# A second table of issue positions, and other engines for a dozen conversions and unit parts, in an mLSTM + MoE kernel

## The chip, the cores and the metric

The kernel runs on one core of one Trainium2 chip. The metric is device microseconds (us) of one execution, median over runs; the profile is one further execution taken by the hardware profiler, and every duration below is from it. Engines: PE (TensorE matmul; PEld its weight loads), DVE (VectorE), ACT (ScalarE), POOL (GpSimd), and SP (SyncE), which here issues DMAs only.

## The reference

Three stages follow one another on 1536 tokens (batch 2 x 768 positions) of width 320 (8 heads x 40).

```
# 1 attention, per batch and head, over t:
m_new = max(f[t] + m, i[t])
C = exp(f[t] + m - m_new) * C + exp(i[t] - m_new) * outer(v[t], k[t])
n = exp(f[t] + m - m_new) * n + exp(i[t] - m_new) * k[t]
y[t] = sigmoid(o[t]) * (C q[t]) / max(|n . q[t]|, 1)
# 2 one dense layer, w_in 320 x 2048, w_out 2048 x 320
h = x @ w_in
g = (a0 + a1 h + a2 h^2 + a3 h^3) / (1 + |b0| |h| + |b1| h^2 + 1e-6)
x = g @ w_out
# 3 four experts, w1 320 x 1024, w2 1024 x 320
out = sum over e of p[:, e] * (relu(x @ w1[e]) @ w2[e])
```

All is float32 outside; the weights of stage 2 arrive as 8-byte values.

## The kernel before, in words

**Attention** is done in 12 tiles (6 chunks of 128 positions x 2 batches). Each tile goes through steps that hang on one another: broadcast of the gates by a matmul (`bc`, `bf`, L415 and L470), a scan over them on DVE (`fb`, L536), the scores `sc` (PE, L566) times that decay (DVE, L571), the chunk's state `dl` (PE, L608 and L611) from `kend` and `v` (POOL and ACT, L554 to L582), the outputs `o` (PE, L590 and L596), a reciprocal of the denominator `den` (DVE, L598, L599 and L624), the output gate (POOL, L627; DVE, L631), and a transpose of the result (`tx`, PE, L651; its high and low halves by ACT L656 and DVE L657). The sigmoid of `o_gate` (tile `so`) is made on ACT from L480 on. All gates are first prepared by `gates1` (L383 to L421), whose scan at L400 needs `f_gate` and `i_gate`.

**The dense layer** is done in 48 units, 6 token groups x 8 pieces of the hidden width; a unit is 16 matmuls into `h` (128x256, L674), the rational function on 128x512 elements (`e_mono`), and 12 matmuls into `acc` (L703). The function takes two ACT operations at L721 and L722, `r = a3 h + a2` (ACT, L724, or DVE, L726), a sum on POOL or DVE (L727), DVE operations at L728, L729, L732, L733 and L734, ACT operations at L730 and L731, and a split of the result `s` into a high part `gh` (ACT, L258) and a low part `gl = s - gh` (L738, POOL or DVE). Every float32 operand of a matmul is split in two parts this way. Strings in the dictionary `KP` name the engine of each of these for each unit (`RI`, `SU`, `GLE`), and where two intermediate results lie (`UP`: P in PSUM, S in SBUF).

**The weights** of the dense layer come in 22 pieces of 512 KB, each a DMA into one of two staging buffers per matrix (`stg_a`, `stg_b`, issued at L315 to L329). A piece is converted from its 8-byte form by ACT (L286, L292), POOL (L298) and DVE (L300), and split into a high part (ACT, L258) and a low part (L267, on POOL or DVE by the string `LO`). The experts' weights are float32, staged as `stg_c` and `stg_d`, split likewise (L258, L262, L267). An expert's unit is 128x512 matmuls into `h`, a relu split on ACT (L743) and DVE (L744), and matmuls into `acc`; the first expert's units are partly laid between units of the dense layer.

**The order.** A step's instructions are traced in the order of emission times in `KP` (`T0`, `ST`, `MT`, `QT` and others). Behind the trace stands the table `ORDER`: for PE, DVE, ACT, POOL and SP a list of ranges of that engine's traced instructions. Each engine's listed instructions are chained in the list's order, so the table, not the trace, sets in what order they are issued; what is behind the table's end follows the scheduler of the framework:

```
for eng, text in ORDER.items():
    own = [i for i in traced if str(i.engine).split(".")[-1] == eng]
    ...
    for a, b in zip(seq, seq[1:]):
        tc.add_manual_dep(b, a.name, ...)
```

Each engine executes its list in order, so an instruction that waits holds up all behind it on that engine.

Of the kernel before, what the change touches and what calls it, by code (L numbers as in the profile page):

```python
# [27 lines left out]
278-293 344 338 345 339 346 340 347 341 348 342 349 343 267-268 306 269 307-309 367 310-325 356-357 350-351 358
352 359 353 360 354 361 355 368-372 389-412 362 413 382 387 421-438 414 383 439 415 388 363 440 384 441 364 442
373 365 416 366 374 443-444 463-478 375 445-446 501 447-448 502 534-539 378 417-418 479-481 419-420 454-458 379  # L30
459-461 380 506 482-497 510-513 449 540-541 498-500 507 542 450 508 543 451 544 452 518-528 509 529-530 453 531
545 532 462 551 533 552 503-505 585 591-592 586 514-517 553 561 554 569 593 570 594 562 555 571 565-568 595 572
563 556 573-574 564 557 575-576 596 558 577 587 578 559 546 579 560 580-582 588 583 589 584 590 630-633 648
547-548 608 634 549 609-610 550 611-612 624 613 625 614-616 597 626 617 635 649 627 618-619 628 600 620-621 601
622-623 602 629 603 598 636 599 637-642 650 643 651-653 604-607 654 662-663 655 684 664 656 665 685 666 657 686
667-668 687 669 688 670-673 689 674 644 675-676 678 677 679-682 645 647 646 683 727-730 696 731 697 732-734 755
698 735 699 736 658-661 700 737-739 718 756 740-741 719 701 742 690 714 691 715 692 716 693 760 694 717 720 761
721 762 695 722 763 723-726 764-766 772-773 767 774-776 708 777 831 709 778 710 779 711 780-781 712 782-785 713
786 832 787 702-707 749-750 743 751 744 833 752 745 834 746 757 768-771 800-802 808 803 809-812 804 813-814 805
815-816 806 817 747 835 807 818 758 748 819 836 820-823 759 753 788 754 794-795 789 837 796 838 797 790 798 839  # L40
791 799 827 792 840 793 828-830 860-861 824 862 825-826 863 892-894 841-856 895-899 857-859 880-891 919-920
864-872 900-901 873-874 902 875-879 925 921 926 922 927 923 928-929 903-916 924 917-918 930 947-948 953-954
949-950 955 951 956-957 952 931-932 958 933-937 959 938 960 939 961 940 962 941 963 942 964 943 965 944 966 945
967 946 968-976 981-982 977-978 983 979 984-985 980 1011-1013 986 1014-1026 987-988 993-994 989-990 995 991
# [12 lines left out]
1390 1318 1339 1391 1340 1392-1393 1341 1394 1324 1395 1342 1396 1343-1344 1347 1345 1348 1346 1369 1349 1370
1350-1351 1375-1376 1371-1373 1352 1374 1377-1380 1435-1436 1397 1419-1426 1400 1427 1401 1428 1398 1402 1429
1441 1403 1430 1399 1442 1431 1404 1437 1432 1405 1438 1433 1406 1434 1407 1439 1408-1412 1463 1443 1413 1464
1414 1465 1440 1415 1466 1469 1467 1470 1444 1471 1445 1472-1473 1468 1475-1477 1474 1478-1479 1446 1416 1480  # L60
1417 1481-1483 1418 1484-1490 1447-1462
    """,
    DVE="""
9-10 8 4 7 5 78 0-3 6 11-12 14 13 40 15 22 24 16 41 23 25 17 43 45 19 18 42 44 20 26-27 21 29 46 31 28 30 32
85-88 36-37 33 38 79 34 39 35 59 63 47 60 57 48 50 80 49 58 61 81 51 82 52 62 68 55 69 72 56 64 73 53-54 65-66
83 91-92 84 67 75 102 70 103 74 71 116 118 99 76-77 130 89 131 133 90 93 120 134 94 121 127 95 128 145 96 129 97
146 100 98 104 101 153 105-106 140-141 107 143 108-109 154 110 132 165 114 111 117 115 112 144 113 142 166 178
122-123 119 147 124 179 125 135 126 136 160 185 137 161 186 138 148 139 149 163 150-151 164 152 155 162 156-159
168 167 169-177 188-191 199 193 192 194 198 180-181 183 195 182 196 184 197 205 217 206 210 218 207 200 187 208
201 209 203 226 211 216 212 204 213 220 214 202 230 215 231 221 219 222 243 242 223-224 232 227 233 225 234 257  # L70
228 235 229 236-237 258 238-241 246 251 264 247 252 244-245 253 248 265 254 249-250 256 255 278 259-260 279
261-262 266 263 267 271 286 270 268 272 287 269 300 273 276 301 274 277 275 281-285 288-289 296 308 297 280 298
290 309 291 299 295 292-294 315-317 302 307 303 318 304-305 319 306 310-311 320 323 312 324 313-314 321 325-326
# [12 lines left out]
245-247 261-264 236 265-266 248 267-268 249 234 252-253 251 254-256 258 269-270 250 259 271 260 272-273 275-277
257 278-279 283-284 274 285 281 286-287 289 280 282 290-291 298 288 295 299 296 292 306 297 307 293 300-302 308
303 294 304 315-316 309-311 305 317 320 312 321-322 313 318 323 319 326 324 314 327-328 332-334 329 325 330
# [10 lines left out]
    """,  # L99
    SP="""  # L100
12 21 13 22 16 14-15 20 17-18 23 28-30 24-26 31 48 47 32-33 49 27 35 19 36-37 44-45 34 38-43 50-51 46 52 61-62
53 63 54 64-65 55-56 66 57-60 92 67-68 96 69 72 70-71 73-81 84 82-83 93-95 97-98
    """,
)


@with_exitstack
def kernel(
# [55 lines left out]
    YB, FB = KP["YB"], KP["FB"]  # L164
# [849 lines left out]
```

## Time and profile before

| | |
|---|---|
| median of 3 runs | 672.76 us (672.57 to 674.09) |
| the profiled execution | 671.89 us, its span 670.1 us |
| PE busy | 624.7 us (93%) |
| DVE busy | 379.1 us (57%) |
| ACT busy | 331.4 us (49%) |
| POOL busy | 233.8 us (35%) |

A row of engine windows gives a stretch, its length, and for each engine the busy time in it (with the count of instructions), then the granted PE clock (1.00 is full speed, 0.50 half), the mean busy share of the DMA engines, and GB/s. A row of a timeline gives start, duration, engine, line, operation, output and input, and in square brackets how long the engine had been idle and what released it. A busy PE need not be a PE at full speed: at half clock a matmul takes twice as long and counts as busy.

In this program the first 100 us hold the start, the conversion of the 22 pieces and the first tiles of attention; from 100 to about 251 us attention's later tiles and the dense layer's units run side by side; from there to about 405 us the dense layer and the first expert; the rest is the other three experts.

### The profile page before, as it was taken

The numbers are of one execution on the slowest core, as the hardware profiler recorded it, in microseconds if no ns is written. First come the engines' busy times: TensorE is split into PE (matmuls) and PEld (weight loads), VectorE is DVE, ScalarE is ACT, GpSimd is POOL, SyncE is SP. The second block draws the span as 40 slices with busy tenths as digits, with TensorE's granted clock in tenths as the row PEclk, the third lists the DMA queues.
The fourth block names the chain that finished last, engine by engine and source line by source line (L and its number), as shares of the span: only waits on it lengthen the run. The fifth ranks groups of instructions, "written<-read, shape, count | busy, mean of one in ns | idle before, by whom it ended". The sixth has DMA issues, their size and how long they took to land.

```text
span 670.1 us, 10411 instructions
## 1 busy us (share of the span) xinstructions
PE 624.7 (93%) x4120; PEld 590.5 (88%) x4120; DVE 379.1 (57%) x615; ACT 331.4 (49%) x618; POOL 233.8 (35%) x225
## 2 busy tenths in 40 slices
PE   2548789999999899999999999999999999999997
PEld 2447779999999899999999999999989999899997
DVE  6887898899988888767665522232222313313232
ACT  3987797876469976857867422111111111111111
POOL 4245677555447752223225994600000000000000
PEclk9568879999999999999999999999999999999999
DMA  8676651012105120000000542000000000001011
GB/s 217 194 196 193 191 161 41 1 53 67 41 1 132 37 87 1 1 1 1 1 1 1 156 143 61 20 1 1 0 1 1 1 0 1 1 1 39 1 40 39
DMA packets 15696, 35.65 MB, mean 53 GB/s; under 512 B 2048, under 2 KB 7424, under 8 KB 15648
## 3 DMA queue, kind: packets, MB, share of 16 engines
q1 hardware_dynamic: 15648, 35.00, 18.1%
q8 instruction: 32, 0.52, 0.3%
q14 instruction: 16, 0.13, 0.1%
HBM read 33.03 MB, written 1.97 MB: 52 GB/s over the span
## 4 chain that ended last, share of the span: by engine, by line
PE 81%; ACT 5%; POOL 4%; DVE 4%; issue 3%; DMA 3%; SPq 0%; DVEq 0%; ACTq 0%; POOLq 0%
PE h L674 38%; PE acc L703 35%; PE sc L566 2%; PE o L596 2%; DMA so<-in_o_gate_dram 2%; DMA stg_a<-in_moe_w_in_dram 1%; PE o L590 1%; PE tx L651 1%; PE dl L611 1%; DVE fb L536 1%; POOL gl L738 1%; ACT cv_l L292 1%; DVE win L267 0%; POOL cv_l L298 0%; PE dl L608 0%
## 5 line engine op out<-in xcount | busy, mean ns | idle before, releaser
L674 PE MATMUL h<-x,we 128*128 128x512 f32 (+1 forms) x960 | 201.7, 348 | 0.0
L744 DVE SCALAR_TENSOR_TENSOR gl<-h,gh 128x512 fp32r<-128x512 f32 x96 | 66.3, 691 | 217.5 <-ACT gh L743 216.4
L674 PEld LDWEIGHTS h<-x,we 128*128 128x128 f32 x960 | 158.2, 189 | 18.7
L743 ACT ACTIVATE gh<-h 128x512 fp32r<-128x512 f32 x96 | 57.4, 598 | 231.7 <-PE h L674 157.2
L703 PE MATMUL acc<-we,gh 128*128 128x320 f32 x768 | 159.0, 309 | 0.0
L703 PEld LDWEIGHTS acc<-we,gh 128*128 128x128 f32 x768 | 126.9, 188 | 5.1
L674 PE MATMUL h<-x,win 128*128 128x256 f32 x768 | 124.1, 290 | 1.9 <-ACT fm L458 1.8
L674 PEld LDWEIGHTS h<-x,win 128*128 128x128 f32 x768 | 107.5, 194 | 3.3 <-ACT x L656 2.1
L703 PE MATMUL acc<-we,gl 128*128 128x320 f32 x384 | 102.6, 309 | 0.0
L703 PE MATMUL acc<-wout,gh 128*128 128x320 f32 x384 | 89.5, 315 | 1.6 <-ACT gh L258 1.6
L703 PEld LDWEIGHTS acc<-we,gl 128*128 128x128 f32 x384 | 68.2, 188 | 0.1
L703 PEld LDWEIGHTS acc<-wout,gh 128*128 128x128 f32 x384 | 63.9, 189 | 2.3 <-ACT gh L258 2.0
L703 PE MATMUL acc<-wout,gl 128*128 128x320 f32 x192 | 57.4, 320 | 0.9 <-POOL gl L738 0.9
L566 PE MATMUL sc<-qkt 128*128 128x128 f32 x192 | 35.6, 316 | 19.2 <-DVE ga L386 12.1
L566 PEld LDWEIGHTS sc<-qkt 128*128 128x128 f32 x192 | 30.8, 223 | 20.8 <-DVE ga L386 12.0
L703 PEld LDWEIGHTS acc<-wout,gl 128*128 128x128 f32 x192 | 35.3, 189 | 1.8 <-POOL gl L738 1.3
L596 PE MATMUL o<-v,fb 128*128 128x41 f32 x192 | 29.1, 289 | 2.5 <-DVE x L657 2.5
L596 PEld LDWEIGHTS o<-v,fb 128*128 128x128 f32 x192 | 28.6, 217 | 2.8 <-DVE x L657 2.7
L536 DVE TENSOR_TENSOR_SCAN fb<-bf,id 128x512 f32<-128x512 f32 x20 | 24.3, 1213 | 2.4 <-PE bf L470 2.4
L267 POOL TENSOR_TENSOR we<-stg_c,we 128x1024 fp32r<-128x1024 f32 (+1 forms) x13 | 24.8, 1920 | 0.8 <-ACT we L258 0.3
L892 DVE SCALAR_TENSOR_TENSOR so<-acc,pr,so 128x320 f32<-128x320 f32 x36 | 17.3, 544 | 2.8 <-PE acc L703 2.8
L267 POOL TENSOR_TENSOR we<-stg_d,we 128x960 fp32r<-128x960 f32 (+1 forms) x9 | 18.7, 2087 | 0.1
(757 smaller groups left out, 905.4 us busy)
## 6 DMA issues: line engine op xcount, KB each, us to landing
stg_b<-in_moe_w_out_dram SPq DMA_DIRECT2D x10, 512.0 KB
stg_a<-in_moe_w_in_dram SPq DMA_DIRECT2D x8, 512.0 KB
stg_c<-in_moe_w_dram SPq DMA_DIRECT2D x8, 512.0 KB
kv<-in_kv_dram SPq DMA_DIRECT2D x12, 320.0 KB
qkt<-in_qk_dram SPq DMA_DIRECT2D x24, 160.0 KB
stg_d<-in_moe_w_dram SPq DMA_DIRECT2D x8, 480.0 KB
stg_a<-in_moe_w_in_dram SPq DMA_DIRECT2D x8, 256.0 KB
stg_c<-in_moe_w_dram SPq DMA_DIRECT2D x8, 256.0 KB
```

Source lines behind the costliest of these rows:

```text
L267: eng.tensor_tensor(out=dst, in0=src, in1=hi.bitcast(F32), op=ALU.subtract)
L292: A.activation(o, i_, AF.Copy, scale=0.9375 / 32)
L536: V.tensor_tensor_scan(W, src, id4f, 0.0, op0=ALU.mult, op1=ALU.add)
L566: PE.matmul(sc[j][:, p, :], qkt[b][:, p, 2 * j], qT[:, p], start=True, stop=True)
L590: PE.matmul(o4[:, p], st["qc"][:, p, :], cold[:, p, :].rearrange("r (j d) -> r j d", j=2), start=(p == 0), stop=False)
L596: PE.matmul(o[:, h, :], st["W"][:, h, :], v1[:, h, :], start=(c == 0 and h == 0), stop=(h == H - 1))
L611: PE.matmul(dl[:, p, :].rearrange("r (j d) -> r j d", j=2), kend[:, p].rearrange("s j d -> s (j d)"), v4[:, p], start=(not ce or c == 0), ...
L674: PE.matmul(o, w5[:, j, fs], r, start=(n == 0), stop=(n == len(seq) - 1))
L703: m = PE.matmul(acc[t], x, y, start=(first and a == 0 and n == 0), stop=(last and a == nff - 1 and n == 2))
L743: A.activation(gh, hp, AF.Relu)
L744: V.scalar_tensor_tensor(out=gl, in0=hp, scalar=0.0, in1=gh.bitcast(F32), op0=ALU.max, op1=ALU.subtract)
L892: V.scalar_tensor_tensor(out=oa, in0=acc, scalar=sc, in1=oa, op0=ALU.mult, op1=ALU.add)
```

## The change

The code is the same, and 40 lines longer by the new table, so line 674 of before is line 714 of after. Two things differ. The table `ORDER` is another one and reaches further: on PE 2437 listed positions instead of 1491, on DVE 524 instead of 414, on ACT 542 instead of 428, on POOL 191 instead of 168, on SP 106 instead of 99. And `KP` has other emission times and other engines:

```diff
-        UP='PPPPPPPPPPPPPPPPPPSPPPPPPPPPPSSSSSSSPPPPPPPSPPPP',
+        UP='PPPPPPSSPPPPPPPPPPSPPPPPPPPPPSSSSPSSPPPPPPPSSPPS',
-        GLE='GGGGGGGGGGGGGGGGGGGGGGGGGGGGGGGGGGGGGGGVVGVGGVVV', L3='AAAAAAAAAAAAAAAAAAAAAA', ...
+        GLE='GGGGGGGGVVVVGGGGGGGGGGGGGGGGGGGGGGGGGGGVVGVGGVVV', L3='AAAAAAAAAAAAAAGAAAAAAA', ...
-        LO='VVGVVGVVGVVGVVGVVGVVGG', ...
+        LO='VVGVVGVVGVVGVVVVVGVVVV', ...
-        ke='AGGGGGGGGGGA', xe='VVVVVVVVVVVV', ...
+        ke='AGGGGGGGAGGA', xe='VVVVVVVVVVVQ', ...
-        LAGB=4, MP=4.9, LEAD=5, XR=0.69, XE=2, E0S=-6.11, E0P=2.33,
+        LAGB=4, MP=4.78, LEAD=5, XR=0.69, XE=2, E0S=-6.11, E0P=2.33,
-        E1S=2.92, eh0='AAAGGG', el0='VGVVVV', eh1='GAAGGG', ...
+        E1S=2.92, eh0='AAAAAG', el0='VGGGVV', eh1='GGGGGG', ...
-        T0=[0.00, 4.33, 20.46, 30.61, 40.08, 50.10, 60.12, 70.14, 77.33, 88.63, 98.40, 109.69],
+        T0=[1.01, 5.30, 21.38, 31.49, 40.92, 50.89, 60.87, 70.85, 78.03, 89.28, 99.83, 111.08],
-        RI='AAAAAAAAAAAAAAAAAAAAAAAAAAAAAAAAAAAAAAAAAAAAAAAA', ...
+        RI='AAAAAAAAAAAAAAAAAAAAAAAAAAVAAVVVVVVVVAAAAAAAAAAA', ...
...
```

(V is DVE, A is ACT, G is POOL.) In words: the low part `gl` of the 9th to 12th unit goes from POOL to DVE; the low parts of pieces 14, 20 and 21 (counted from 0) go from POOL to DVE, and one integer step of piece 14 from ACT to POOL; `r` of nine units (the 27th, and the 30th to 37th) goes from ACT to DVE; two of the intermediate results lie in SBUF instead of PSUM in four more units, and in PSUM instead of SBUF in one; of the weights of the first expert two high parts move from POOL to ACT and two low parts from DVE to POOL, of those of the second two high parts from ACT to POOL; three smaller parts of attention tiles change engines.

What the new table does to the issue order is shown at three places. The first is SP's queue at the program's start (`ga` is the gates' tile, `stg_a` and `stg_b` the staged weight pieces, `so` the output gate). Before:

```order
L203 DMA ga<-in_f_gate_dram 16x768
L315 DMA stg_a<-in_moe_w_in_dram 128x1024
L204 DMA ga<-in_i_gate_dram 16x768
L315 DMA stg_a<-in_moe_w_in_dram 128x1024
L240 DMA kv_161<-in_kv_dram 128x640
L238 DMA qkt_117<-in_qk_dram 40x4x256 x2
L246 DMA so<-in_o_gate_dram 128x640
L238 DMA qkt_118<-in_qk_dram 40x4x256 x2
L246 DMA so<-in_o_gate_dram 128x640 x4
L317 DMA stg_a<-in_moe_w_in_dram 64x1024
L318 DMA stg_a<-in_moe_w_in_dram 64x1024
L329 DMA stg_b<-in_moe_w_out_dram 128x1024
```

And now:

```order
L243 DMA ga<-in_f_gate_dram 16x768
L244 DMA ga<-in_i_gate_dram 16x768
L355 DMA stg_a<-in_moe_w_in_dram 128x1024 x2
L280 DMA kv_161<-in_kv_dram 128x640
L278 DMA qkt_117<-in_qk_dram 40x4x256 x2
L286 DMA so<-in_o_gate_dram 128x640
L278 DMA qkt_118<-in_qk_dram 40x4x256 x2
L286 DMA so<-in_o_gate_dram 128x640
L357 DMA stg_a<-in_moe_w_in_dram 64x1024
L358 DMA stg_a<-in_moe_w_in_dram 64x1024
L369 DMA stg_b<-in_moe_w_out_dram 128x1024
L286 DMA so<-in_o_gate_dram 128x640 x4
```

The load of `i_gate` moved one place ahead, and three of the `so` loads, with the last one, moved behind the third piece of `w_in` and the first of `w_out`.

The second place is ACT's queue in the same stretch (`win` is the high part of a weight piece, `cv_t` and `cv_l` its conversion, `cm` the masked gates that the first broadcast needs). Before:

```order
L383 ACTIVATE ga<-ga 48x128
L286 ACTIVATE cv_t<-stg_a 128x512
L292 ACTIVATE cv_l<-stg_a 128x512 x2
L286 ACTIVATE cv_t<-stg_a 128x512
L384 ACTIVATE ga<-ga 48x128
L480 ACTIVATE so<-so 128x640
L258 ACTIVATE win<-cv_t 128x512 x2
L480 ACTIVATE so<-so 128x640
L405 ACTIVATE ga<-ga 48x128
L554 ACTIVATE v_0_221<-kv_161,ist 128x40
L408 ACTIVATE cm<-ga,mask 48x128 x4
```

And now:

```order
L423 ACTIVATE ga<-ga 48x128
L326 ACTIVATE cv_t<-stg_a 128x512
L332 ACTIVATE cv_l<-stg_a 128x512
L424 ACTIVATE ga<-ga 48x128
L326 ACTIVATE cv_t<-stg_a 128x512
L298 ACTIVATE win<-cv_t 128x512
L332 ACTIVATE cv_l<-stg_a 128x512
L298 ACTIVATE win<-cv_t 128x512
L445 ACTIVATE ga<-ga 48x128
L520 ACTIVATE so<-so 128x640
L448 ACTIVATE cm<-ga,mask 48x128 x4
```

The gates' last activation (L405, now L445) and the masks `cm` now stand behind one activation of `so`, not two, and the first weight pieces' high parts are ahead of it.

The third place is DVE's queue at the 9th and 10th unit of the dense layer (`s__1286` and `s__1338`, now `s__1285` and `s__1337`, are their results; `den`, `fb`, `qc` and `x` belong to attention). Before:

```order
L728 TENSOR_TENSOR r__1340<-h,r__1340 128x512
L734 SCALAR_TENSOR_TENSOR s__1286<-h,r__1288 128x512
L729 SCALAR_TENSOR_TENSOR r__1340<-r__1340,a_t,h 128x512
L571 TENSOR_TENSOR fb_1237<-sc_0_1250,fb_1237 128x512
L598 TENSOR_SCALAR den_1223<-o_1125 128x8
L599 SCALAR_TENSOR_TENSOR den_1223<-o_1125,den_1223 128x8
L624 RECIPROCAL den_1223<-den_1223 128x8
L732 SCALAR_TENSOR_TENSOR r__1340<-r__1340,a_t,h 128x512
```

And now:

```order
L768 TENSOR_TENSOR r__1339<-h,r__1339 128x512
L774 SCALAR_TENSOR_TENSOR s__1285<-h,r__1287 128x512
L769 SCALAR_TENSOR_TENSOR r__1339<-r__1339,a_t,h 128x512
L778 TENSOR_TENSOR gl<-s__1285,gh 128x512
L772 SCALAR_TENSOR_TENSOR r__1339<-r__1339,a_t,h 128x512
L773 SCALAR_TENSOR_TENSOR h<-s__1337,h 128x512
L638 TENSOR_SCALAR den_1389<-o_1315 128x8
L774 SCALAR_TENSOR_TENSOR s__1337<-h,r__1339 128x512
```

The low part `gl` stands one operation behind the product that it is made from, ahead of the next unit's L772, and the attention work around it is that of a later tile (`o_1315` instead of `o_1125`).

## Rows read from the trace of the kernel before

**Rows 1.** The page: busy time per engine, and the chain that ended last.

```profile
PE 624.7 (93%) x4120; PEld 590.5 (88%) x4120; DVE 379.1 (57%) x615; ACT 331.4 (49%) x618; POOL 233.8 (35%) x225
...
PE 81%; ACT 5%; POOL 4%; DVE 4%; issue 3%; DMA 3%; SPq 0%; DVEq 0%; ACTq 0%; POOLq 0%
```

**Rows 2.** Engine windows: stretch, length, busy per engine, PE clock, DMA share, GB/s.

```profile
0.00:21.00 21.00, 4.66 (x19) 4.31 (x20) 13.16 (x32) 9.45 (x22) 7.17 (x18) 0.94 0.89 221
21.00:100.00 79.00, 56.80 (x331) 51.52 (x330) 70.09 (x118) 67.64 (x138) 46.01 (x58) 0.73 0.62 185
100.00:134.00 34.00, 33.96 (x262) 33.20 (x261) 28.35 (x49) 27.68 (x50) 22.95 (x24) 1.00 0.08 23
134.00:184.00 50.00, 49.78 (x400) 48.28 (x400) 47.08 (x83) 32.79 (x74) 26.09 (x33) 1.00 0.18 54
184.00:251.00 67.00, 63.91 (x486) 61.90 (x485) 57.43 (x92) 54.61 (x98) 42.20 (x33) 1.00 0.25 64
251.00:405.00 154.00, 154.00 (x1171) 153.80 (x1170) 95.17 (x137) 94.97 (x165) 70.37 (x49) 1.00 0.13 38
405.00:670.10 265.10, 261.62 (x1463) 237.51 (x1461) 67.82 (x109) 44.24 (x75) 19.03 (x13) 1.00 0.03 10
```

**Rows 3.** Timeline of the first 22 us, rows of SP, DVE and ACT.

```profile
1.64 0.43 SPq L204 DMA_DIRECT2D ga<-in_i_gate_dram  x1
...
6.09 0.71 DVE L400 TENSOR_TENSOR_SCAN gb<-ga 16x128 f32<-16x128 f32 x1 [1.64 <-DMA ga<-in_i_gate_dram]
...
7.18 4.10 SPq L246 DMA_DIRECT2D so<-in_o_gate_dram  x4
...
13.32 0.74 ACT L480 ACTIVATE so<-so 128x640 f32<-128x640 f32 x1 [2.15 <-DMA so<-in_o_gate_dram]
...
17.49 0.74 ACT L480 ACTIVATE so<-so 128x640 f32<-128x640 f32 x1 [2.39 <-DMA so<-in_o_gate_dram]
...
18.77 1.28 ACT L408 ACTIVATE cm<-ga,mask 48x128 fp32r<-48x128 f32 x4
...
20.93 1.22 DVE L536 TENSOR_TENSOR_SCAN fb<-bc,id 128x512 f32<-128x512 f32 x1 [1.19 <-PE bc L415]
```

**Rows 4.** The chain in order of time, 60 to 95 us: start, length, what.

```profile
75.61 5.06 DMA stg_a<-in_moe_w_in_dram
```

**Rows 5.** Engine windows around 90 us, columns as above.

```profile
83.40:87.40 4.00, 0.56 (x2) 0.18 (x1) 3.24 (x8) 3.65 (x7) 4.00 (x4) 0.94 0.43 131
87.40:93.05 5.65, 5.59 (x22) 5.03 (x23) 5.56 (x10) 4.85 (x11) 3.16 (x5) 0.50 0.61 186
93.05:100.00 6.95, 6.95 (x56) 6.91 (x54) 6.92 (x11) 6.74 (x14) 5.85 (x8) 0.95 0.52 154
```

**Rows 6.** Low parts of weight pieces: DVE by tile (min/median/max ns), POOL by group.

```profile
L267 DVE TENSOR_TENSOR win<-cv_t,win x7: 684/691/1134, 14.6 to 90.4; 128x512 fp32r<-128x512 f32 x5, 64x512 fp32r<-64x512 f32 x2
...
L267 POOL TENSOR_TENSOR wout<-cv_t,wout 128x512 fp32r<-128x512 f32 x4 | 5.1, 1275 | 0.3 <-ACT wout L258 0.3
```

**Rows 7.** Timeline of DVE and POOL where `gl` is already on DVE, 319 to 374 us.

```profile
319.10 0.69 DVE L738 TENSOR_TENSOR gl<-s__3481,gh 128x512 fp32r<-128x512 f32 x1 [1.68 <-ACT gh L258]
...
365.85 0.69 DVE L728 TENSOR_TENSOR r__4085<-h,r__4085 128x512 f32<-128x512 f32 x1 [2.54 <-ACT r__4085 L724]
...
368.11 1.29 POOL L727 TENSOR_TENSOR s__4083<-s__4083,u__4084 128x512 f32<-128x512 f32 x1
368.26 1.70 DVE L738 TENSOR_TENSOR gl<-s__4001,gh 128x512 fp32r<-128x512 f32 x1 [0.93 <-ACT gh L258]
```

**Rows 8.** Waits of PE from 100 us on: line, releaser, us in total, times, longest.

```profile
PE acc L703 <- ACT gh L258: 1.6, 2, 0.8
PE acc L703 <- POOL gl L738: 0.9, 2, 0.5
```

**Rows 9.** Timeline around 400 us: the second expert's last weight conversion, its first matmuls.

```profile
389.48 2.42 POOL L267 TENSOR_TENSOR we<-stg_c,we 128x1024 fp32r<-128x1024 f32 x1
...
404.49 1.77 PE L674 MATMUL h<-x,we 128*128 128x512 f32 x7
```

More of the change, by code (lines that the diff above doesn't have):

```diff
@@ L28 @@
[L28 to L32, printed above, removed]
@@ L58 @@
[L58 to L61, printed above, removed]
+5-9 2 10-12 0 3-4 1 13 21 25-28 22-23 29 24 30 14 31 15 32 16-20 33-47 71-80 131 48-53 132 54 136-139 55-70
+81-90 97-100 91 122 92-93 123 94-96 124-128 140 129 141-143 101-105 178 130 133-135 179 183 144-147 169-176
@@ new lines @@
+184-187 106-121 207-218 188 164-168 265 189-190 177 266 270-273 180-182 219-222 256-263 274-277 375 148-163
+244-245 250-251 246-248 252-254 249 255 223 376 224-225 264 226-227 380-386 267-269 306-309 366-372 387 373
+362-365 500-501 191-206 294-295 300-301 374 296-298 302-303 299 304-305 505-508 228-243 326-327 332 328 333
+329-330 334-336 331 337 509-511 377-379 416 278-293 338-339 344 340 345 341-342 346-348 343 349 417-419 310-325
+388-398 350 399 351 400-401 356 402 357 403 352-354 358-360 355 361 404 420-435 405-415 453-455 448 512 456
@@ new lines @@
+1106-1109 1084 1110-1113 1120-1121 1114-1119 1126-1127 1122-1123 1085-1103 1124 1128-1130 1125 1131 1148-1149
+1154-1155 1150-1152 1156 1153 1157-1161 1132-1147 1176-1177 1182-1183 1178-1180 1184-1186 1181 1187 1162-1167
+1188-1203 1216 1168 1217 1169 1218 1170 1219 1171 1220 1172 1221 1173 1222 1174 1223 1204 1175 1224 1205 1225
+1210 1226 1206 1211 1227 1207 1228-1229 1208 1212 1230 1213 1231 1214 1209 1232 1215 1238 1233 1239 1234 1240
+1235 1241 1236 1242 1237 1243-1246 1260 1247-1248 1261 1266 1249 1267 1250-1251 1262 1252 1263 1253 1264 1268
@@ new lines @@
+1254 1269 1255-1256 1270 1257 1324 1258 1265 1272-1274 1271 1275 1288 1294 1276 1289 1259 1277 1295 1278-1285
+1290 1286 1296 1291 1287 1297 1292 1298 1300-1301 1306-1307 1302 1325 1293 1303 1326 1299 1304 1308 1327 1309
+1328 1352 1310 1329-1330 1305 1331 1353 1332 1354 1333 1355 1311 1334 1356 1335 1357 1336 1358 1337 1359 1338
+1360 1339 1361-1367 1380-1390 1399 1391 1312 1400 1392 1401 1313 1393 1318 1402 1319 1403 1314 1394 1404 1395
+1315 1405 1316 1320-1322 1317 1323 1406-1409 1340 1346 1410 1341 1347 1411 1342 1412 1348 1343 1413-1414 1349
@@ new lines @@
+1344 1350 1368-1369 1345 1351 1370-1379 1434-1435 1396-1398 1440 1436 1441 1437 1442 1438 1443-1444 1462 1439
+1463 1468-1469 1445 1415-1417 1464 1470 1418-1433 1465 1471 1466 1472 1467 1473 1446 1474-1483 1447 1484 1448
+1485 1449 1486-1487 1502-1513 1450 1488 1451 1496 1490 1489 1452 1497 1491 1453-1454 1524 1518 1455 1514 1525
+1519 1456 1515 1457 1516 1458 1517 1492 1459 1493 1460-1461 1494 1498-1500 1520 1526 1521 1527 1522 1528 1495
+1501 1523 1529 1552 1546 1553 1547 1530-1538 1558-1560 1548 1554 1561 1549 1555 1562 1550 1556 1563-1567 1551
@@ new lines @@
+1729 1710-1711 1730-1732 1712 1733 1713 1734-1735 1714 1736 1715 1737-1743 1694-1699 1716 1700 1717 1701 1766
+1702 1767 1703-1704 1768 1718 1705 1719-1720 1706-1707 1721 1708-1709 1744-1748 1769-1773 1749 1774 1750 1775
+1751 1776 1752 1777 1753 1778 1754 1779 1755 1810 1780 1756 1811 1781-1782 1757 1783 1758 1784 1759-1761
+1812-1814 1804 1815 1805 1785-1786 1762 1787 1763-1764 1806-1807 1765 1788 1808 1789-1792 1809 1793-1796 1866
+1797-1798 1867 1799-1803 1832 1816 1838 1833 1817 1839 1868 1818 1869 1819 1834 1820 1870 1835 1844 1821 1840
```

166 lines of the change are left out of this document (94 added, 72 removed).

## The prediction

> **What bounds the kernel now.** I read the page's totals first: PE is busy 93% of the span and carries 81% of the chain that ended last [rows 1]. So nearly all that can change is time in which PE waits, or runs at half clock. The windows by stage say where that is [rows 2]. In the first 21 us PE works 4.66 us, in the next 79 us 56.80. That is 38.5 us of PE idle in 100 us, and the granted clock there is 0.73. From 100 us on PE idles 0.04, 0.22, 3.09, 0 and 3.48 us in the five stretches: 6.8 us in 570. So the onset decides, and whatever it gains has to be carried through 100 to 251 us, where PE has nothing to spare and another engine can become late. There DVE is busy 28.35 of 34, 47.08 of 50 and 57.43 of 67 us: it idles 5.65, 2.92 and 9.57 us, while PE is full.
>
> The timeline of the first 22 us shows what the onset hangs on [rows 3]. The scan at L400 starts when `i_gate` has landed (6.09 us), ACT waits twice for a load of `so` (until 13.32 and 17.49 us), the masks `cm` come behind that, and the first decay scan L536 starts at 20.93 us. Later the chain lies on a landing weight piece, 5.06 us from issue [rows 4]; and around 85 us there is a hole, PE working 0.56 of 4 us, behind which it runs 5.65 us at half clock [rows 5].
>
> **The change part by part.** The sums are made against the profiled execution, 671.89 us; the median of the runs is 672.76, 0.87 us more, and the result is moved by that.
>
> *The start.* `i_gate` is issued one place earlier, where the first `stg_a` load was, so about 0.45 us before its 1.64. The masks now stand behind one `so` activation, whose load is at the same place of SP's queue as before: it can be done at 13.32 + 0.74 = 14.06 us, and `cm` may follow. The gates' other inputs (L425, L426, L445, L446, with two weight pieces between them) reach the same point by DVE and ACT work of about 14.2 us when I lay the rows' durations one behind another. From `cm` to the scan was 20.93 - 18.77 = 2.16 us. So the scan starts at about 16.4, or at 17.1 with a few small waits: 3.8 to 4.5 us earlier. I take -4.0. The four `so` loads that took 4.10 us to issue now stand behind the third piece of `w_in` and the first of `w_out`, so these are converted earlier too, and the sigmoids later; the outputs need `so` only at the first tile's end.
>
> *The middle of the onset, 21 to 100 us.* ACT and DVE are busy 67.64 and 70.09 of 79 us, and pieces land 5.06 us after issue through two buffers. The new order cannot make pieces land faster. Here the low parts of pieces 14, 20 and 21 come onto DVE, 0.69 us each by the median, 1.13 by the longest, against 1.28 on POOL [rows 6]. That is 2.1 to 3.4 us more of DVE. Before 100 us DVE has 7.84 us of idle in the first 21 and 8.9 in the rest. In the stretch where pieces 20 and 21 are converted, 87.40 to 100, it is busy 12.48 of 12.60 us [rows 5]: no cover. I take one of the three as on the path with a small wait, +0.9 us; bounds 0 and +3.4. Below nothing: the hole of 83.40 to 87.40 (3.44 us idle) and the half clock behind it (5.59 us busy at 0.50, so 2.8 us lost) could close, -6.2 us; a table that lays attention's tiles earlier bears on just that, but the hole ends with DVE's and ACT's work, which grows on DVE. I take no gain from it and keep the end for the range.
>
> *The four `gl` on DVE.* DVE takes 4 operations. Where a unit has its `gl` on DVE already, it took 0.69 us at 319.10, with 1.68 us of idle before it for `gh`, and 1.70 us at 368.26 with 0.93 us of idle before it, while POOL worked on L727 [rows 7]. In the new order one operation (L769) stands between the product and `gl`, so the wait for `gh` is mostly covered, and what is queued behind is the next unit's L772 and with it PE's second half of that unit. Price: 4 x 0.69 = 2.8 us at least, 4 x 1.70 = 6.8 at most, without waits. DVE's idle in 100 to 184 us is 5.65 + 2.92 = 8.57 us. So by count it fits, and I take +0.3 us on the path (a short hole or two); bounds -0.5 (PE waited 0.9 us for POOL's `gl` in all [rows 8]) and +6.8.
>
> The longer `gl` at 368.26 has its neighbour on POOL, of two SBUF inputs like itself, from 368.11 to 369.40: the two ran one behind the other [rows 7]. The Trainium skill, SBUF — State Buffer, section "SBUF: two separate sides", says that VectorE with two SBUF inputs and GpSimd share a port pair as an exclusive lock, held for the whole instruction, so the later one is blocked. The trace agrees: 1.70 us beside POOL's operation, 0.69 without one. By that rule a moved `gl`, and the products of the 7th and 8th unit, whose factors now lie in SBUF, cost DVE up to POOL's 1.29 us more whenever POOL is in L727; by the count of the short ones alone, nothing of that. It speaks against the change; what it would do here is the second rival.
>
> *`r` of nine units from ACT to DVE.* The time of this form on DVE does not stand in the trace; the nearest row of the same tile size with one PSUM input is L728, 0.69 us [rows 7]. Bounds 0.5 and 0.8, so 4.5 to 7.2 us of DVE between 250 and 330 us, where it idles 154 - 95.17 = 58.8 us [rows 2]. Hidden: PE works 154.00 of 154 us there. If the cover were gone, each would cost 0.69. It can't gain either, for PE cannot be fuller.
>
> *The experts' weights.* Two high parts more on POOL for the second expert. Before, the last low part ended at 389.48 + 2.42 = 391.90 us and the first matmul that reads these weights began at 404.49 [rows 9]: 12.6 us of room, where a 128x1024 high part on POOL is less than the 2.42 of that low part. Hidden. Two parts of the first expert's weights that move between ACT, DVE and POOL, and the three small attention parts, are likewise work of engines that idle more than 9 us between 184 and 251 us; nothing.
>
> *The longer table.* From 251 to 405 us PE is full [rows 2]. A fixed order there can only hold or lose; bounds 0 and +2, taken +0.2. The holes of 3.09 us in 184 to 251 us are the one thing left to gain there: attention's tiles stand earlier in PE's order and the dense layer's units behind them can fill. I take -0.4, as DVE is the reason for them and has more to do.
>
> Sum: -4.0 + 0.9 + 0.3 + 0.2 - 0.4 = -3.0 us, 668.9 us for the profiled execution, 669.8 us against the median. A change under 0.3% (2.0 us) can't be told from none here: faster is below 670.7, slower above 674.8.
>
> **The rivals.**
>
> *The lead is absorbed.* Pieces go through two buffers, and DMA's share in the first 21 us is 0.89 [rows 2]: the lead of 4 us may be lost when the next piece isn't there, and the onset ends where it did. For it speaks the 5.06 us piece on the chain [rows 4]; against it that the share is 0.62 from 21 us on and that the later chain there is mostly DVE's and ACT's. Time: 671.9 - 4.0 + 4.0 + the 0 to 1 us of the other terms, 672.8 to 673.5 on the median.
>
> *DVE becomes the bound from 100 to 251 us.* One mechanism: the operations moved from POOL to DVE, each blocked while POOL is busy. DVE gets 4 `gl` of up to 1.70 us and the low parts of pieces 20 and 21 of up to 1.13 [rows 6, 7]: 9.06 us, while its idle time where they fall is 0.12 us (87.40 to 100 [rows 5]) and 2.92 (134 to 184 [rows 2]). It decides when the added DVE time there is over these 3.04 us plus the 4.0 us of lead: 9.06 - 7.04 = +2.0 us at the longest durations, and the wait for `gh` in front of each (0.93 in the row, four times 3.7) makes it up to +5.7. So 674.8 to 678.5, middle 676. For it: PE has full work, DVE 94% of that stretch, and the longer `gl`. Against: 8.57 us of idle from 100 to 184 us, and units that run several ahead of what DVE delivers, as PE waits of 0.9 us in all show.
>
> *The hole at 85 us closes as well.* If the three to four us of lead persist and attention's tiles reach PE before the pieces end, PE has work in 83.40 to 87.40 us and stays at full clock: -3.0 - 6.2 = -9.2 us, or half of it; 663.6 to 667. For it: the hole is released by attention's DVE work, which moved ahead. Against: PE's idle time before 100 us is 38.5 us in many holes, and a closed one opens another as long as DVE is busy 70.09 of 79 us.
>
> **How the numbers follow.** The forecast 0.40, the closed hole 0.16, the absorbed lead 0.20, DVE as the bound 0.24. That the change doesn't do what it says is out: the issue order shows the moves. Of the forecast's 0.40 (its own range 667.5 to 672) a quarter, 0.10, lies within 0.3%; of the absorbed lead 0.14 within, 0.02 below and 0.04 above; of the DVE case 0.05 within and 0.19 above; the closed hole is all faster. Faster 0.48, within 0.3% 0.29, slower 0.23. The range 664.5 to 676.5 leaves out about one in ten on either side.
>
> **What would show it right or wrong.** Right: the first L536 scan (now L576) between 16 and 17.2 us; PE's idle time before 100 us 3 us lower at the same busy clock; DVE 48 to 50 us busy in any 50 us stretch between 100 and 184 us without PE waits above 1 us in sum; no idle PE from 251 to 405 us. Wrong: the scan no earlier, since some load of the start landed later; holes of PE in 100 to 240 us released by DVE's `gl` or products, several times 0.5 us; a `gl` on DVE of 1.2 us or more in each of the four units; or a clock of 1.00 where it was 0.50 around 90 us, which would make the gain some 6 us larger.

## The result, and the profile after

| | before | changed |
|---|---|---|
| median | 672.66 us | 680.11 us (678.48 to 681.23, 4 runs) |
| ratio to before | | 1.0112 (95%: 1.0092 to 1.0131) |
| profiled execution, its span | 671.89, 670.1 us | 680.87, 679.1 us |
| PE busy | 624.7 us | 630.6 us |

The changed kernel is 1.1% slower: 7.5 us by the medians, 9.0 us by the two profiled executions. The forecast was 669.8 us, and its range ended at 676.5. The windows of the changed kernel, with the stretches and columns of [rows 2], show where:

```profile
0.00:21.00 21.00, 5.20 (x21) 4.26 (x21) 17.15 (x35) 14.04 (x33) 8.80 (x21) 0.91 0.87 250
21.00:100.00 79.00, 63.28 (x352) 57.82 (x353) 67.09 (x119) 60.65 (x123) 42.39 (x56) 0.74 0.60 178
100.00:134.00 34.00, 32.79 (x259) 31.95 (x257) 31.23 (x52) 27.71 (x48) 22.26 (x24) 1.00 0.14 40
134.00:184.00 50.00, 49.94 (x393) 48.32 (x393) 48.09 (x86) 35.90 (x85) 21.68 (x26) 1.00 0.15 41
184.00:251.00 67.00, 63.72 (x492) 62.70 (x491) 58.43 (x92) 56.79 (x101) 43.20 (x33) 1.00 0.26 64
251.00:405.00 154.00, 145.04 (x1084) 144.23 (x1083) 108.50 (x140) 84.07 (x150) 70.77 (x50) 0.97 0.12 36
405.00:679.10 274.10, 270.59 (x1530) 246.38 (x1528) 69.22 (x111) 46.65 (x79) 19.05 (x13) 1.00 0.04 11
```

Ahead of 100 us PE is idle 31.5 us (15.80 + 15.72) instead of 38.5: the onset gained, and more than the 3 us of idle time that the forecast had named. From 100 to 251 us it is idle 4.55 us instead of 3.35. In the stretch that was full before, 251 to 405 us, it is idle 8.96 us. PE's waits from 100 us on, as in [rows 8], say that this is one wait:

```profile
PE acc L743 <- ACT gh L298: 9.0, 1, 9.0
PE acc L743 <- POOL gl L778: 1.7, 1, 1.7
PE h L714 <- issue: 1.6, 1, 1.6
PE h L714 <- DVE s__834 L774: 1.2, 1, 1.2
```

The timeline of DVE and POOL around it (the last rows are ACT's, DVE's and PE's):

```profile
361.82 1.26 DVE L778 TENSOR_TENSOR gl<-s__3959,gh 128x512 fp32r<-128x512 f32 x1
...
363.00 1.53 DVE L778 TENSOR_TENSOR gl<-s__4006,gh 128x512 fp32r<-128x512 f32 x1
...
365.47 2.99 POOL L307 TENSOR_TENSOR we<-stg_c,we 64x512 fp32r<-64x512 f32 x2
365.70 1.62 DVE L772 SCALAR_TENSOR_TENSOR r__4090<-r__4090,a_t,u__4089 128x512 f32<-128x512 f32 x1
367.24 12.73 DVE L773 SCALAR_TENSOR_TENSOR s__4088<-s__4088,u__4089 128x512 f32<-128x512 f32 x1
368.44 0.99 POOL L302 TENSOR_SCALAR we<-stg_d 128x960 fp32r<-128x960 f32 x1
369.39 1.05 POOL L302 TENSOR_SCALAR we<-stg_c 128x1024 fp32r<-128x1024 f32 x1
370.40 2.39 POOL L307 TENSOR_TENSOR we<-stg_c,we 128x1024 fp32r<-128x1024 f32 x1
372.75 4.37 POOL L307 TENSOR_TENSOR we<-stg_d,we 128x960 fp32r<-128x960 f32 x2
377.08 2.34 POOL L307 TENSOR_TENSOR we<-stg_c,we 128x1024 fp32r<-128x1024 f32 x1
380.00 0.69 DVE L774 SCALAR_TENSOR_TENSOR s__4088<-s__4088,r__4090 128x512 f32<-128x512 f32 x1
...
380.81 0.63 ACT L298 ACTIVATE gh<-s__4088 128x512 fp32r<-128x512 f32 x1 [15.75 <-DVE s__4088 L774]
...
381.49 1.17 PE L743 MATMUL acc<-wout,gh 128*128 128x320 f32 x3 [8.96 <-ACT gh L298]
```

A DVE operation that takes 0.69 us elsewhere is recorded as 12.73 us long. It belongs to the 48th and last unit of the dense layer, whose intermediate results the change moved to SBUF, so both its inputs lie there. It begins while POOL splits the second expert's weights, and ends at 379.97 us, 0.55 us after POOL's last operation of that run (377.08 + 2.34 = 379.42). It is the only one held so long: in the same rows L772, also with two SBUF inputs, took 1.62 us, and the two `gl` ahead of it 1.26 and 1.53. PE, whose next matmuls in its order need the product, waits 8.96 us, and then runs at half clock for a while (PE is the first busy column, the clock the third number from the end):

```profile
372.50:381.50 9.00, 0.04 (x2) 0.01 (x1) 8.19 (x3) 0.69 (x2) 6.92 (x4) 0.66 0.70 186
381.50:384.00 2.50, 2.50 (x9) 2.50 (x10) 1.26 (x2) 0.42 (x1) 0.00 (x0) 0.50 0.41 143
384.00:386.00 2.00, 2.00 (x10) 1.96 (x10) 0.54 (x1) 1.18 (x3) 0.85 (x1) 0.58 0.00 0
```

2.5 us at 0.50 and 2.0 us at 0.58 lose 1.25 + 0.84 = 2.1 us (the 128x320 matmuls start 0.27 us apart there, 0.15 before the wait). Wait and clock together are 11 us, more than the whole difference of 9.0: the rest of the change gained about 2 us in this execution, and 3.6 by the medians (11.1 - 7.5).

### The profile page after: what moved, and what is told of

Read it like the earlier page. It is cut to its first block, busy times and chain, and to the rows that moved or that the text cites. A ratio compares the mean times of both kernels' runs of the same rounds, so it can differ in the third digit from the quotient of the medians.

```text
span 679.1 us, 10402 instructions
## 1 busy us (share of the span) xinstructions
PE 630.6 (93%) x4118; PEld 595.7 (88%) x4118; DVE 399.7 (59%) x630; ACT 325.8 (48%) x614; POOL 228.2 (34%) x220
## 4 chain that ended last, share of the span: by engine, by line
PE 82%; DVE 8%; issue 3%; ACT 3%; POOL 2%; DMA 1%; SPq 0%; DVEq 0%; ACTq 0%; POOLq 0%
PE h L714 38%; PE acc L743 36%; PE sc L606 2%; PE o L636 2%; DVE s__4088 L773 2%; DMA stg_a<-in_moe_w_in_dram 1%; PE tx L691 1%; PE o L630 1%; PE dl L651 1%; POOL we L307 1%; DVE fb L611 1%; DVE fb L576 1%; DVE win L307 1%; ACT cv_l L332 0%; POOL gl L778 0%
## 5 line engine op out<-in xcount | busy, mean ns | idle before, releaser
L714 PE MATMUL h<-x,we 128*128 128x512 f32 (+1 forms) x960 | 218.9, 349 | 1.6 <-issue 1.6
L714 PEld LDWEIGHTS h<-x,we 128*128 128x128 f32 x960 | 166.9, 189 | 20.4 <-issue 1.8
L783 ACT ACTIVATE gh<-h 128x512 fp32r<-128x512 f32 x96 | 57.4, 598 | 233.9 <-PE h L714 148.4
L743 PE MATMUL acc<-we,gh 128*128 128x320 f32 x768 | 163.5, 310 | 0.0
L743 PEld LDWEIGHTS acc<-we,gh 128*128 128x128 f32 x768 | 128.4, 189 | 5.2
L714 PE MATMUL h<-x,win 128*128 128x256 f32 x768 | 126.7, 291 | 3.2 <-DVE s__651 L774 1.9
L714 PEld LDWEIGHTS h<-x,win 128*128 128x128 f32 x768 | 109.9, 196 | 5.2 <-DVE s__651 L774 2.2
L743 PE MATMUL acc<-wout,gh 128*128 128x320 f32 x384 | 94.5, 320 | 9.0 <-ACT gh L298 9.0
L743 PEld LDWEIGHTS acc<-wout,gh 128*128 128x128 f32 x384 | 66.2, 193 | 10.3 <-ACT gh L298 9.6
L606 PEld LDWEIGHTS sc<-qkt 128*128 128x128 f32 x192 | 31.0, 230 | 22.5 <-issue 17.1
L307 POOL TENSOR_TENSOR we<-stg_c,we 64x512 fp32r<-64x512 f32 (+1 forms) x15 | 27.4, 1832 | 0.9 <-PE h L714 0.3
L307 POOL TENSOR_TENSOR we<-stg_d,we 128x960 fp32r<-128x960 f32 (+1 forms) x10 | 20.4, 2043 | 0.2
```

What stands on the lines that cost most here:

```text
L307: eng.tensor_tensor(out=dst, in0=src, in1=hi.bitcast(F32), op=ALU.subtract)
L606: PE.matmul(sc[j][:, p, :], qkt[b][:, p, 2 * j], qT[:, p], start=True, stop=True)
L714: PE.matmul(o, w5[:, j, fs], r, start=(n == 0), stop=(n == len(seq) - 1))
L743: m = PE.matmul(acc[t], x, y, start=(first and a == 0 and n == 0), stop=(last and a == nff - 1 and n == 2))
L783: A.activation(gh, hp, AF.Relu)
```

## The experiments

In most of them the rows of one unit decide, the 48th: its operations L772, L773 and L774 and its low part `gl` (L778). Lines that an edit adds or cuts shift the numbers behind them: with the pause these four are L775, L776, L777 and L781, with the two high parts on ACT L776, L777, L778 and L783, and with the product in PSUM L774 and L778 become L775 and L779.

**Its intermediate results back in PSUM.**

```diff
-UP='PPPPPPSSPPPPPPPPPPSPPPPPPPPPPSSSSPSSPPPPPPPSSPPS'
+UP='PPPPPPSSPPPPPPPPPPSPPPPPPPPPPSSSSPSSPPPPPPPSSPPP'
```

> The changed kernel, with the two intermediate results of the 48th unit back in PSUM; everything else, the issue order too, as in the changed kernel. Theory A (in the changed kernel L773 of the 48th unit, both of whose inputs lay in SBUF, was held 12.73 us while POOL ran eight operations on the second expert's weights; PE lost the 8.96 us of its wait and about 2 us at half clock behind it): L773 takes 0.7 us, PE works through 372 to 382 us, and the time is 680.1 - 10.9 = 669 us, 3 to 4 us below the kernel before. Rival B (POOL's eight operations hold up what the end of the dense layer needs, whatever the DVE operands): the wait stays, 678 to 681 us. Rival C (the rest of the change loses too): the wait goes, but the time is 672 to 674 us.

Measured: 677.40 us, ratio 1.0080 (1.0066 to 1.0095), so none of the three. The timeline of DVE in it:

```profile
363.85 0.74 DVE L772 SCALAR_TENSOR_TENSOR r__4090<-r__4090,a_t,h 128x512 f32<-128x512 f32 x1
364.51 0.69 DVE L773 SCALAR_TENSOR_TENSOR h<-s__4088,h 128x512 f32<-128x512 f32 x1
365.23 0.69 DVE L774 SCALAR_TENSOR_TENSOR s__4088<-h,r__4090 128x512 f32<-128x512 f32 x1
...
366.70 11.14 DVE L778 TENSOR_TENSOR gl<-s__4088,gh 128x512 fp32r<-128x512 f32 x1 [0.78 <-ACT gh L298]
```

The three operations, which now read one input from PSUM, take 0.7 us beside POOL's `we` operations; the next one with two SBUF inputs, `gl`, is held 11.14 us in their place, until 0.55 us after POOL's last operation, and PE waits 6.8 us for it. The mechanism was confirmed, but I had looked at one operation of the unit only.

**Both inputs in SBUF, the output in PSUM.**

```diff
-UP='...SSPPS'
+UP='...SSPPE'
```

(E: the first intermediate result, an input of L772 and L773, stays in SBUF; the result of L773 goes to PSUM.)

> The changed kernel, but L773 of the 48th unit writes its result to PSUM; both its inputs stay in SBUF. L774 then reads one operand from PSUM and one from SBUF. Theory A1 (what holds the operation is that both inputs are in SBUF): L773 is still held about 12 us, 679 to 681 us. Rival A2 (it is the write to SBUF, or the output in the place of an input): L773 takes 0.7 us, about 669 us.

680.21 us in a single run, and L773 is as long as before the edit. Where its result goes made no difference:

```profile
366.64 12.76 DVE L773 SCALAR_TENSOR_TENSOR h<-s__4088,u__4089 128x512 f32<-128x512 f32 x1
```

**No DVE operation of the unit with two SBUF inputs.** To the first edit this adds that the product itself lies in PSUM:

```diff
+        s = hp if k == 47 else s
         V.scalar_tensor_tensor(out=s, in0=e, scalar=2.0, in1=r, ...)
```

> The changed kernel without the added wait, with the 48th unit's two intermediate results and its final product in PSUM: no DVE operation of that unit has two SBUF inputs any more, its gl reads PSUM and SBUF. The issue order is the changed one. Theory A (the number of SBUF inputs decides): no DVE operation of this unit is longer than 0.8 us beside POOL's operations, PE has no wait for it, 667 to 669.5 us, as with the gap in POOL's work. Rival A7 (any DVE operation that has to read what ACT or DVE wrote to SBUF is held there): one of them is held over 5 us, 676 to 680 us.

668.21 us, ratio 0.9938 (0.9916 to 0.9961). Nothing is held, though POOL's run is the same:

```profile
365.68 0.70 DVE L775 SCALAR_TENSOR_TENSOR h<-h,r__4090 128x512 f32<-128x512 f32 x1
366.71 0.99 POOL L302 TENSOR_SCALAR we<-stg_d 128x960 fp32r<-128x960 f32 x1
367.12 0.69 DVE L779 TENSOR_TENSOR gl<-h,gh 128x512 fp32r<-128x512 f32 x1 [0.74 <-ACT gh L298]
367.67 1.05 POOL L302 TENSOR_SCALAR we<-stg_c 128x1024 fp32r<-128x1024 f32 x1
```

Of these three kernels and the changed one together: no operation of the unit with an input in PSUM was held, and where the unit had operations with two inputs in SBUF, one of them was held until POOL's run ended. The changed kernel's whole trace says the same of the inputs, but not that a hold must be long: of 144 DVE operations on two 128x512 operands, at least one of them in PSUM, that ran beside a POOL operation for over 0.2 us none took over 0.75 us; of 34 with both in SBUF one took 12.73 us, and the next longest 1.86.

**A pause in POOL's run.** All as in the changed kernel, with one wait added on POOL:

```diff
...
+            tc.add_manual_dep(HOLD["pool"], seq[at - 2].name, ...)
```

(`HOLD["pool"]` is POOL's low part of one piece, the operation at 370.40 us in the changed kernel; it waits for a PE matmul just ahead of those that need the 48th unit's product.)

> The changed kernel, results of the 48th unit in SBUF as there; one wait is added: POOL's third-last group of low parts of the second expert's weights (the operation that began at 370.40 us) waits until PE has done its last matmul before the 48th unit's second half (at about 372 us). This leaves POOL idle for 1 to 2 us in the middle of its eight operations. Theory A3 (the held DVE operation gets in as soon as POOL has an idle moment): L773 ends within 1 us of POOL's gap, about 371 us, PE's wait falls from 8.96 us to under 1.5 us, 669 to 671 us. Rival A4 (the held operation waits for something that has nothing to do with POOL's stream): L773 stays 12 us long, 680 us; with POOL 1.7 us later it could be 682.

668.00 us in a single run. More runs were to settle whether that was chance:

> The changed kernel with the one added wait on POOL, timed. If the one look at 668.0 us was right: 667 to 669.5 us, 3 to 5 us below the kernel before, which is what the start's 4 us leaves when the held operation is gone. If it was chance: 670 to 673 us.

668.29 us, ratio 0.9933 (0.9915 to 0.9950). The timeline of one of these:

```profile
365.82 2.74 DVE L776 SCALAR_TENSOR_TENSOR s__4088<-s__4088,u__4089 128x512 f32<-128x512 f32 x1
367.02 1.00 POOL L302 TENSOR_SCALAR we<-stg_d 128x960 fp32r<-128x960 f32 x1
367.98 1.48 POOL L302 TENSOR_SCALAR we<-stg_c 128x1024 fp32r<-128x1024 f32 x1
368.59 1.41 DVE L777 SCALAR_TENSOR_TENSOR s__4088<-s__4088,r__4090 128x512 f32<-128x512 f32 x1
...
371.04 2.69 POOL L307 TENSOR_TENSOR we<-stg_c,we 128x1024 fp32r<-128x1024 f32 x1 [1.58 <-PE h L716]
```

POOL pauses 1.58 us, DVE's operations are 1.4 to 2.7 us long, and PE has no wait for this unit. The hold thus comes from POOL's stream, and PE loses nothing by POOL's later end. One thing went otherwise than expected: L776 ended at 368.56, before the pause, between two POOL operations of which the second took 1.48 us instead of 1.05. So DVE can get in between two operations. In the changed kernel the same end of a POOL operation (368.44 + 0.99 = 369.43) passed without it. So the pause acted before POOL stood idle: DVE got in one POOL operation ahead of it.

**Two high parts of the second expert back on ACT.**

```diff
-eh1='GGGGGG'
+eh1='GAAGGG'
```

(The two stand behind the 47th unit's `gh` in ACT's queue.)

> The changed kernel, with two high parts of the second expert's weights (128x1024) back on ACT, as in the kernel before; the 48th unit's results stay in SBUF, the rest of the order is the changed one. POOL's low parts of these two then wait for ACT. Theory A5 (a DVE operation of two SBUF inputs is held while POOL's operations follow each other with no wait on another engine; all six high parts on POOL made that run): the longest DVE operation of the 48th unit is under 5 us, PE waits under 3 us for it, 668 to 672 us. Rival A6 (POOL's amount of work alone counts, here 2.1 us less of some 14): L773 is held 9 to 11 us, 677 to 680 us.

679.22 us, ratio 1.0096 (1.0076 to 1.0116). Theory A5 fell: the operation ahead of the one held before (L772 by the numbers of the changed kernel, L776 here) was held in its place, and nearly as long, although POOL's run now contained a wait on ACT. ACT had finished its two parts at 363.06 us, and the POOL operation that reads one of them began at 367.17, right behind the one ahead of it. A wait that was already fulfilled was no pause:

```profile
364.20 12.57 DVE L776 SCALAR_TENSOR_TENSOR r__4090<-r__4090,a_t,u__4089 128x512 f32<-128x512 f32 x1
```

**Each edit alone on the kernel before.** First the 48th unit's results in SBUF:

```diff
-UP='...PPPPPPPSPPPP',
+UP='...PPPPPPPSPPPS',
```

> The kernel before, with one edit: the two intermediate results of the 48th unit in SBUF instead of PSUM. In its profile POOL works from 369.37 to 374.32 and from 374.40 to 379.76 us on the second expert's weights, and L732 to L734 of that unit stood at 370.83 to 372.9. Theory A (an operation of two SBUF inputs can be held for as long as POOL's operations follow one another): one of L732 to L734 is held for 3.5 to 9 us, PE waits for it, and the time is 675 to 683 us. Rival D (a held operation gets in at the next end of a POOL operation, as 1.2 to 1.9 us in the rows of before): each is under 2.5 us long, no wait of PE above 2 us, 672 to 675 us.

676.92 us in a single run, 4.8 above the kernel before in that series. Two operations were held 2.8 and 3.2 us, each under the 3.5 of the one expectation and over the 2.5 of the other; PE's longest wait for them is 1.8 us:

```profile
372.51 2.76 DVE L733 SCALAR_TENSOR_TENSOR s__4083<-s__4083,u__4084 128x512 f32<-128x512 f32 x1
...
377.73 3.24 DVE L738 TENSOR_TENSOR gl<-s__4083,gh 128x512 fp32r<-128x512 f32 x1 [0.76 <-ACT gh L258]
```

Then all six high parts of the second expert on POOL:

```diff
-eh1='GAAGGG'
+eh1='GGGGGG'
```

> The kernel before, with one edit: all six high parts of the second expert's weights on POOL (two were on ACT). The scheduler moves a few operations around it. Theory A5: the low part gl of the 48th unit, two SBUF inputs on DVE, is held through POOL's run, 5 to 12 us, and the time is 677 to 682 us. Rival (the position of the 48th unit's results is needed too): gl under 3.3 us, 671 to 674 us.

674.45 us in a single run, 1.9 above the median of before, whose 17 runs reach from 670.47 to 674.31, so the time alone says little. `gl` was held 4.52 us, under the 5 that I had put and over the rival's 3.3. First its row here, then the same `gl` in the kernel before:

```profile
375.54 4.52 DVE L738 TENSOR_TENSOR gl<-s__4083,gh 128x512 fp32r<-128x512 f32 x1 [0.76 <-ACT gh L258]
```

```profile
373.66 1.21 DVE L738 TENSOR_TENSOR gl<-s__4083,gh 128x512 fp32r<-128x512 f32 x1 [0.76 <-ACT gh L258]
```

Neither edit alone makes a hold of 11 us. In the kernel before, `gl` got in at the end of the POOL operation then running (374.32 us). What decides at which end of a POOL operation DVE gets in, and at which it doesn't, I could not settle.

**The start undone.** The kernel with the pause, but SP's first loads and ACT's first 30 operations in the order of before:

```diff
 Activation:
-0 8-9 1 11 10 12-13 2 7 3-6 22-29 72
+0 8-9 12 11 1 7 10 13 72 2 22 3-6 23-29
 SP:
-12-13 21-22 16 14-15 20 17-18 23-26 28-31
+12 21 13 22 16 14-15 20 17-18 23 28-30 24-26 31
```

> The kernel of the added POOL wait, with the first part of two queues as in the kernel before: SP's order of the first 19 loads and ACT's first 30 operations; all else as in the changed kernel. Theory S (the start carries the gain): the first scan L576 starts at about 20 us instead of 15.5, and the time is 3.5 to 5.5 us above that of the added wait alone, 671.5 to 673.5 us. Rival S2 (the start's lead is absorbed before 100 us, the gain comes from the later order): within 1 us of it, 667 to 669 us.

674.31 us, 6.0 above the 668.29 of the same series and more than the 3.5 to 5.5 expected: the start carries the gain, and nothing of it is absorbed. Against the kernel before this is a ratio of 1.0030 (1.0015 to 1.0046): without the new start and without the hold, the rest of the change costs about 1.8 us. The first decay scan (L561 in this kernel) was back at 20.61 us:

```profile
18.47 1.26 ACT L433 ACTIVATE cm<-ga,mask 48x128 fp32r<-48x128 f32 x4
...
20.61 3.45 DVE L561 TENSOR_TENSOR_SCAN fb<-bc,id 128x512 f32<-128x512 f32 x3 [0.82 <-PE bc L440]
```

**`gl` of the 9th to 12th unit back on POOL,** with the pause:

```diff
-GLE='GGGGGGGGVVVVGGGG...'
+GLE='GGGGGGGGGGGGGGGG...'
```

> The kernel of the added POOL wait, with gl of the 9th to 12th unit back on POOL (behind the next unit's L727, as the kernel before has it); DVE 2.8 us less to do. Theory G (the four gl cost next to nothing, +0.3 us in the prediction): within 1 us of 668.3 us. Rival G2 (DVE is the bound from 100 to 184 us and they cost 2 us or more): 665 to 666.5 us. Rival G3 (POOL would be late with them, so the move gains): 669.5 to 672 us.

667.63 us, ratio 0.9935 (0.9915 to 0.9956) against 0.9933 with the four on DVE: no difference that can be told.

**The 7th and 8th unit's results back in PSUM,** with the pause:

```diff
-UP='PPPPPPSSPPPP...'
+UP='PPPPPPPPPPPP...'
```

> The kernel of the added POOL wait, with the intermediate results of the 7th and 8th unit in PSUM, as in the kernel before. Theory U (the SBUF places cost there what held operations show in the trace, under 1 us): within 1 us of 668.3 us. Rival U2 (they free PSUM for the next units' matmuls and so gain): 669.5 to 672 us, with PE waits for the units 9 or 10. Rival U3 (held DVE operations cost PE time): 665 to 667 us.

677.70 us, ratio 1.0085 (1.0057 to 1.0113): 1.5% above the pause alone, far more than any of the three. PE's waits from 100 to 250 us name the reason:

```profile
PE h L716 <- DVE s__1147 L777: 4.4, 1, 4.4
PE h L716 <- DVE s__1088 L777: 2.1, 1, 2.1
```

In PSUM the two units' results keep the `h` buffer until the product L777 has read it, and the next matmuls into that buffer wait for it. This order of issue needs the SBUF placement there; it lets PE run ahead, while the same placement in the 48th unit made three operations more that POOL could hold. The two waits are 6.5 of the 9.4 us; most of the rest is PE's clock behind them, 0.57 from 124 to 128 us and 0.72 from 136 to 140, where it was full in the kernel with the pause.

**The two mends together, without a pause.** The 48th unit all in PSUM and the four `gl` on POOL, both edits as above.

> The changed kernel without an added wait, with two edits together: the 48th unit's results and product in PSUM, and gl of the 9th to 12th unit back on POOL. If the two do not touch each other: no held operation in the 48th unit, 667 to 668.5 us, 4 to 5 us below the kernel before. If four more operations on POOL bring a hold back elsewhere: over 669 us with a PE wait above 2 us from 100 us on.

668.44 us, ratio 0.9929 (0.9910 to 0.9948), with no wait of PE above 1.7 us from 100 us on. The time is inside the stretch expected, at its upper end. It can't be told from the 48th unit's placement alone (ratio 0.9938): four `gl` that cost nothing give nothing back. All four mended versions lie 0.6 to 0.7% below the kernel before and 1.7 to 1.8% below the changed one.

## Why the prediction was wrong

*The step that failed* is the term of the longer table, from 251 to 405 us, "bounds 0 and +2, taken +0.2", and with it the word "Hidden" for the experts' weights. The term measured 8.96 us of wait and about 2 us at half clock behind it. I had asked whether the weights would be ready in time (12.6 us of room [rows 9], and indeed PE waited for none of them; by the order of the loads issued behind each, the row read there is already the third expert's, and the second's last low part ended at 386.14 us, so the room was 18.4 us), and not which DVE operation would run beside POOL while it made them. For the placement of intermediate results in SBUF (`UP`) the sum had no term at all, and the 48th unit is not named in the prediction.

*The blocked DVE operation* was right as a mechanism, and I looked for it at the wrong units. The runs show what is subject to it: an operation with two SBUF inputs, held 11.14 to 12.76 us in four kernels; with one input in PSUM, 0.7 us at the same place. The Trainium skill, SBUF — State Buffer, section "SBUF: two separate sides", says that the one of the two engines that comes later is blocked while the other's instruction holds the shared pair. The runs agree, and in them the next POOL operation could come ahead of the blocked one again. My price for it was one POOL operation of 1.29 us, because the one row that I had taken showed that [rows 7]. The runs show that the price can be the whole run of POOL operations that follow each other: six or seven of them here. The same trace would have shown the risk: at 368 to 375 us DVE's two `gl` took 1.70 and 1.21 us beside POOL's weight splits, and the change brought three more two-input operations (L772 to L774 of the 48th unit) and more POOL work to that place.

*The rival "DVE becomes the bound"* had the blocking and the sign, but in the wrong stretch and for other operations: what was held had been on DVE before, and only its inputs had moved. From 134 to 184 us DVE was busy 48.09 us and PE idle 0.06; the four moved `gl` took 0.68 to 0.69 us each, and moving them back changed nothing. The term of +0.3 us was right within what can be measured.

*The start* was forecast at -4.0 us and is worth 6.0 by the run that undoes it. The scan came at 15.52 us, not at 16.4 to 17.1. The timeline of the changed kernel, to be held against [rows 3]:

```profile
1.18 0.41 SPq L244 DMA_DIRECT2D ga<-in_i_gate_dram  x1
...
3.58 0.40 DVE L440 TENSOR_TENSOR_SCAN gb<-ga 16x128 f32<-16x128 f32 x1
...
11.39 0.72 ACT L520 ACTIVATE so<-so 128x640 f32<-128x640 f32 x1
...
12.51 1.28 ACT L448 ACTIVATE cm<-ga,mask 48x128 fp32r<-48x128 f32 x4 [0.39 <-DVE ga L446]
...
15.52 3.43 DVE L576 TENSOR_TENSOR_SCAN fb<-bc,id 128x512 f32<-128x512 f32 x3
```

`i_gate`, issued 0.46 us earlier, was there 2.5 us earlier (the scan that needs it moved from 6.09 to 3.58 us, and stood at 6.05 again in the run that undoes the start), and the first `so` did not make ACT wait. I had moved landings by what the issue moved; here a 48 KB load that no longer had a 512 KB one ahead of it gained 2.5 us for 0.46 us of issue.

*The rival of the absorbed lead* fell, by the start undone. *The hole at 83 to 87 us* shrank, as the third rival said it could: from 83.40 to 87.40 us PE works 2.80 of 4 us, at clock 1.00, where it worked 0.56 [rows 5]. Three shorter holes of 0.5 to 0.7 us and one of 1.93 us at 92 us took its place, so its 6 us did not come in full.

Without the held operation the sum was near: -3.0 us forecast; 668.29 against 672.56 us and 668.21 against 671.77 us are -4.3 and -3.6. That is in part luck: two misses cancel. The start gave 6.0 us where 4.0 were forecast, and the other terms together cost 1.8 us where they were put at +1.0; which of them cost more, no run separates, beyond the four `gl`.

## What to carry to other kernels

Where a vector operation with both inputs in SBUF runs beside a long run of GpSimd work, don't price it by its duration elsewhere, and not by one GpSimd operation either: look at how long that run is, and whether PE has other work while the one result is missing. One operand of every such operation in PSUM, or a pause of under 2 us in the GpSimd queue, took the whole loss away here; with one two-input operation left beside the run, that one was held. When work is moved to an engine because it has room, look at what else runs during that time, not only at the deadline of what is moved.

## What the runs showed of the hardware that I had not expected

A DVE operation of 0.69 us can be held for 12.7 us, across seven POOL operations and the ends of the first six, while others in the same trace got in at the first end (1.26 to 1.62 us). The changed order of issue, without a pause, gave a hold of over 11 us in every kernel that kept a two-input operation there. A wait on POOL that was already fulfilled when POOL came to it was no pause for DVE.

The granted clock in the records of the first 100 us differs between executions of one and the same kernel. These two rows are two executions of the kernel with the pause (668.00 and 668.60 us):

```profile
0.00:100.00 100.00, 69.56 (x392) 62.84 (x392) 86.65 (x156) 76.32 (x159) 53.24 (x80) 0.86 0.66 193
```

```profile
0.00:100.00 100.00, 69.76 (x385) 62.30 (x386) 87.31 (x155) 75.59 (x157) 52.35 (x79) 0.95 0.66 193
```

The clock is 0.86 and 0.95, and PE's busy time and the execution's time differ by 0.2 and 0.6 us. The half-clock stretches of the onset, of which I had made a possible gain of 2.8 us, are no sure guide to time there.
